# The opening of a delta-rule and feed-forward kernel, rearranged

## The chip, the cores and the metric

The kernel runs on one core of a Trainium2 chip. The metric is the device time of one execution in microseconds, the median over several executions. Engines are called as the profile calls them: PE (matrix products; PEld is its weight load), DVE (vector), ACT (scalar), POOL (GpSimd) and SP (which only issues DMAs). ACT, POOL and SP each have a DMA queue that they issue to in program order.

## The reference

For 4 batches, 8 heads and 768 steps of 48 dimensions, a delta rule is run over time, and its output goes through a feed-forward layer that takes the maximum of three products:

```python
k_n = k / (np.linalg.norm(k, axis=-1, keepdims=True) + 1e-06)
for t in range(S):
    kt, vt, bt = (k_n[:, :, t], v[:, :, t], beta[:, :, t, None])
    y[:, :, t] = np.einsum('bhd,bhde->bhe', q[:, :, t], state)
    v_old = np.einsum('bhde,bhd->bhe', state, kt)
    state = state + bt[:, :, :, None] * np.einsum('bhd,bhe->bhde', kt, vt - v_old)
...
x = attn_out.transpose(0, 2, 1, 3).reshape(B * S, H * D)      # 3072 x 384
h = np.maximum(np.maximum(x @ w1, x @ w2), x @ w3)            # 3072 x 768
out = h @ w_out                                               # 3072 x 384
```

## The kernel before

**Tiling.** Time is cut into 12 chunks of 64 steps (C = 64), and each chunk into two halves (BL = 32) and four quarters (HB = 16). A chunk has two units of work: unit n holds chunk n // 2 and half of the batches. Four units (two chunks) make a group m, of which there are six; a group is also one tile of 512 tokens of the feed-forward layer. All sums are in 32-bit floats.

**Within a chunk.** The steps depend on each other through a triangular system. `turn` transposes keys (part 0) or queries (part 1) of a unit on PE and evicts them to `kqt`; `gram` multiplies keys by keys (`at`) or keys by queries (`pt`); `keys` is gram of the keys alone. `solve(m)` inverts the diagonal blocks on DVE, one column of all blocks per two instructions (the lines L617 and L621). For group 0 the blocks are quarters of 16, because FINE = 1, and their inverses are then joined to halves of 32 and to the chunk by small products on PE. The order of these, with PE's tile name and line, is

- `halves_z` (p_e, L740): keys times the second quarters of the solution, evicted to z (L743)
- `halves_u` (p_f, L751): t times z, negated into the solution's tile `ut` (L755). t is the solution transposed, made by `halves_t` with three DVE transposes of `ut` (L700, L702)
- `turn_t1` (L685, L687): DVE transposes of the first half, to t1
- `join_z` (p_z, L768) and its evictions (L772), then `join_u` (p_j, L781), negated into `ut` (L783)
- `new` (p_u, L826): the chunk's updates u; `to_y` (p_y, L868): its output y; `to_x` (p_x, L887): y transposed into `xt` (L894), the tokens of the feed-forward layer
- `step` (p_s, L849) with the addition on DVE (L856): the state `st`; `old_k` (p_k, L798) and `old_q` (p_q) of the next chunk multiply by that state.

`heads_of` and `negated_of` deal out a stage's PSUM tiles and the engines that evict them: for chunk 0 in two parts of four heads, for later chunks in one. Their PSUM tiles (`ps_two`) come from a pool of three. `placed(cc, i, copy, part)` copies a block of the transposed solution `xs[0]` into `ut`; part is the first or the second quarter.

**Weights.** The three input weights and the output weight come as 64-bit values and are converted in 24 pieces. `fetch` asks for a piece (384 KB) on a queue; `weights()`, drawn by `some(conv, n)`, makes the two halves of a piece with three ACT instructions (L255 to L257, about 0.5 us each) per draw; `joined` finishes it with a shift on DVE (L266) and an addition on POOL (L270). `join_last` does that for a piece whose ACT part is done.

**Order.** The scheduler is off (`manual_schedule`): every engine's order is the order of the calls in the program. The opening is written out line by line, to the first feed-forward product (p_h, L1303); after it each of the feed-forward layer's products is followed by pieces of the recurrence that tables name. The solution is drawn in steps, `some(solving, n)`: for group 0 one step up to the scaling, 15 columns, and one that transposes and places the result and ends.

`busy(n, ident)` issues n products of the identity that nobody reads (p_w, L1377).

## Time and profile before

| | |
|---|---|
| median of 3 runs | 502.3 us (500.78, 502.30, 502.41) |
| the profiled execution | 501.92 us, of which the span (first to last instruction) is 500.0 us |
| mean granted PE clock | 0.976 |
| PE busy | 480.2 us, 96% of the span |
| DVE, POOL, ACT busy | 348.8, 196.1, 169.6 us |
| the solution of group 0 on DVE (L617, L621) | 16.29 to 25.21 us |
| first feed-forward product (p_h) | starts at 44.06 us |

Times are microseconds from the span's start. A line of the timeline has the start, the busy time, the engine, the source line, the operation with its tiles and shapes, the number of instructions merged into it, and in brackets how long the engine had been idle before it and what ended that. A line of the chain of waits has the start, the length, and the work or wait that led there. A window's line has the length, the busy time of each engine, the granted PE clock (1.00 is full speed) and the share of the DMA engines' time. PE's 32-bit products each leave two records.

### The profile page before, as it was taken

The numbers are of one execution on the slowest core, as the hardware profiler recorded it, in microseconds if no ns is written. First come the engines' busy times: TensorE is split into PE (matmuls) and PEld (weight loads), VectorE is DVE, ScalarE is ACT, GpSimd is POOL, SyncE is SP. The second block draws the span as 40 slices with busy tenths as digits, with TensorE's granted clock in tenths as the row PEclk, the third lists the DMA queues.
The fourth block names the chain that finished last, engine by engine and source line by source line (L and its number), as shares of the span: only waits on it lengthen the run. The fifth ranks groups of instructions, "written<-read, shape, count | busy, mean of one in ns | idle before, by whom it ended". The sixth has DMA issues, their size and how long they took to land.

```text
span 500.0 us, 18781 instructions
## 1 busy us (share of the span) xinstructions
PE 480.2 (96%) x8100; PEld 343.4 (69%) x8100; DVE 348.8 (70%) x819; ACT 169.6 (34%) x329; POOL 196.1 (39%) x330
## 2 busy tenths in 40 slices
PE   7869799999999999999999999999999999999997
PEld 6658688878665556565555565565797457988896
DVE  4888898656697352979552998565998864468753
ACT  5686665985330153201243200252211032212310
POOL 6557684764670394780575870601000020000000
PEclk9767899999999999999999999999999999999999
DMA  8948979874351655543775552833223330330001
GB/s 107 168 100 220 211 178 137 199 218 77 81 144 34 140 117 121 138 126 88 155 129 120 146 135 65 176 50 93 65 68 79 61 72 19 86 77 15 1 16 49
DMA packets 110114, 53.51 MB, mean 107 GB/s; under 512 B 93264, under 2 KB 103920, under 8 KB 110032
## 3 DMA queue, kind: packets, MB, share of 16 engines
q1 hardware_dynamic: 98528, 32.01, 31.8%
q0 software_dynamic: 9088, 19.72, 15.8%
q8 instruction: 64, 1.05, 0.9%
q10 hardware_dynamic: 2416, 0.59, 0.7%
q14 instruction: 18, 0.15, 0.1%
HBM read 39.17 MB, written 13.11 MB: 105 GB/s over the span
## 4 chain that ended last, share of the span: by engine, by line
PE 88%; DVE 3%; DMA 2%; ACT 2%; issue 2%; POOL 1%; SPq 1%; DVEq 0%; POOLq 0%; ACTq 0%
PE p_h L1303 34%; PE p_o L1346 13%; PE p_o L1040 10%; PE p_g L443 5%; PE p_c L1241 4%; PE p_u L826 3%; PE p_y L868 3%; PE p_k L798 2%; PE p_m L960 2%; PE p_t L366 2%; PE p_q L798 2%; PE p_s L849 2%; PE p_j L781 2%; PE p_z L768 2%; PE p_e L1241 1%
## 5 line engine op out<-in xcount | busy, mean ns | idle before, releaser
L1303 PE MATMUL p_h<-xt,w_sb 128*128 128x512 f32 (+1 forms) x468 | 177.7, 523 | 0.6 <-ACT xt L894 0.3
L1303 PEld LDWEIGHTS p_h<-xt,w_sb 128*128 128x128 f32 x468 | 85.1, 191 | 62.0 <-issue 53.0
L1317 DVE TENSOR_TENSOR h<-h,p_h 128x512 f32<-128x512 f32 (+1 forms) x42 | 23.9, 569 | 55.9 <-PE p_h L1303 53.4
L617 DVE TENSOR_TENSOR tmp<-x_bl,y_bl 128x31 f32<-128x31 f32 (+20 forms) x139 | 50.3, 362 | 4.0
L621 DVE TENSOR_TENSOR y_bl<-y_bl,tmp 128x31 f32<-128x31 f32 (+20 forms) x139 | 46.5, 334 | 4.8
L1346 PE MATMUL p_o<-wo_sb,h 128*128 128x384 f32 x144 | 49.2, 490 | 0.4 <-POOL wo_sb L270 0.4
L1313 ACT ACTIVATE h<-p_h 128x512 f32<-128x512 f32 (+1 forms) x30 | 16.6, 552 | 76.2 <-PE p_h L1303 76.2
L401 POOL DMA_DIRECT2D turned<-in_q_dram x72 | 39.2, 552 | 5.1 <-POOL turned L396 2.6
L1346 PEld LDWEIGHTS p_o<-wo_sb,h 128*128 128x128 f32 x144 | 26.8, 190 | 18.5 <-POOL wo_sb L270 1.0
L443 PEld LDWEIGHTS p_g<-kqt 48*64 48x64 f32 x1184 | 23.5, 138 | 11.5 <-issue 7.1
L443 PE MATMUL p_g<-kqt 48*64 48x64 f32 (+1 forms) x1184 | 26.7, 238 | 2.9 <-ACT kqt L372 2.9
L270 POOL TENSOR_TENSOR w_sb<-mant,up 128x384 int32<-128x384 int32 x18 | 18.5, 1032 | 23.7 <-DVE mant L266 20.0
L1352 ACT COPY o_sb<-p_o 128x384 f32<-128x384 f32 x12 | 5.7, 478 | 61.7 <-PE p_o L1346 41.7
L396 POOL MEMSET turned<- 128x96 f32 x18 | 3.3, 190 | 59.1 <-DVE kqt L417 59.1
L653 POOL DMA_DIRECT2D ut<-y_d x4 | 2.6, 651 | 60.4 <-DMA y_d<-y_bl 60.4
L148 POOL DMA_DIRECT2D v_t<-in_v_dram x14 | 11.6, 830 | 28.7 <-PE p_u L826 28.7
L856 DVE TENSOR_TENSOR st<-st,p_s 48x768 f32<-48x768 f32 (+1 forms) x18 | 17.1, 951 | 7.7 <-PE p_s L849 7.3
L810 DVE TENSOR_TENSOR v_t<-v_t,p_k 128x768 f32<-128x768 f32 x11 | 10.4, 949 | 15.3 <-PE p_k L798 15.3
L1346 PE MATMUL p_o<-w_sb,xt 128*128 128x384 f32 x60 | 21.0, 486 | 0.0
L427 DVE TENSOR_TENSOR pt<-p_g,mask 128x512 f32<-128x512 f32 x20 | 13.7, 689 | 10.4 <-PE p_g L443 10.3
L460 ACT COPY at<-p_g 128x512 f32<-128x512 f32 x22 | 12.7, 583 | 18.8 <-DVE pt L427 16.5
L401 POOL DMA_DIRECT2D turned<-in_k_dram x32 | 17.5, 553 | 3.0 <-DMA v_t<-in_v_dram 1.9
(252 smaller groups left out, 917.4 us busy)
## 6 DMA issues: line engine op xcount, KB each, us to landing
w_bits<-in_moe_w_dram SPq DMA_DIRECT2D x9, 384.0 KB, 5.3
w_bits<-in_moe_w_dram POOLq DMA_DIRECT2D x9, 384.0 KB, 4.8
turned<-in_q_dram POOLq DMA_DIRECT2D x72, 48.0 KB, 2.6
out_dram<-o_sb SPq DMA_DIRECT2D x34, 96.0 KB, 2.3
y_x<-y SPq DMA_DIRECT2D x32, 96.0 KB, 2.3
qall<-y_x SPq DMA_DIRECT2D x32, 96.0 KB, 2.9
v_t<-in_v_dram POOLq DMA_DIRECT2D x14, 192.0 KB, 4.5
at_d<-at SPq DMA_DIRECT2D x76, 32.0 KB, 2.9
```

The costliest lines, as they stand in the source:

```text
L270: nc.gpsimd.tensor_tensor(out=dst.bitcast(I32), in0=mant_v.bitcast(I32), in1=up_v, op=ALU.add)
L401: (queue, nc.gpsimd)[i].dma_start(out=t[p0 : p0 + 32, bb, at : at + NP * 2 * D].rearrange("p (j x) -> p j x", j=NP), in_=(k, q)[i][2 * bb ...
L443: nc.tensor.matmul(p_g[rows(bb ^ (g * i)), par, c0 : c0 + C * (1 + whole)], kq[:, 0], kq if whole else kq[:, i],)
L617: nc.vector.tensor_tensor(out=t_v, in0=row.to_broadcast(t_v.shape), in1=column.to_broadcast(t_v.shape), op=ALU.mult,)
L621: nc.vector.tensor_tensor(out=rest, in0=rest, in1=t_v, op=ALU.subtract)
L798: nc.tensor.matmul(p_b[rows(bb), par, c0 : c0 + D], kqt[g][dims(par), j, bb ^ g, i], st[dims(par), bb ^ g, g, j],)
L856: nc.vector.tensor_tensor(out=s_v[r], in0=s_v[r], in1=p_s[r, :, 0 : H * D], op=ALU.add)
L1040: nc.tensor.matmul(to[:, g], a[j][:, 128 * g : 128 * (g + 1)], b[j], start=(start and g == of[0] and j == 0), stop=(stop and g == of[-1] a ...
L1241: nc.tensor.matmul(to, w[stays], moves, start=(n == 0), stop=(n == len(terms) - 1))
L1303: nc.tensor.matmul(p_h, w_sb[i][:, t, f * 128 : (f + 1) * 128], xt[:, t, lo : lo + w], start=(t == 0), stop=(t == KT - 1),)
L1317: nc.vector.tensor_tensor(out=h, in0=h, in1=p_h, op=ALU.max)
L1346: nc.tensor.matmul(p_o, stays, moves, start=(n == 0), stop=(n == len(terms) - 1))
```

## The change

It concerns the opening (group 0) alone, but for the way conversions are drawn and for the products of `join_z` in chunk 1.

- t of chunk 0 is no longer made by transposing `ut`. One DVE transpose of the solution itself (`corners`, into the free tile t1[1]) gives the first quarters, and eight small copies (`corner`) put them into t, which POOL has cleared before: three on DVE, three on POOL, two on ACT. The second quarter of `ut` is placed first (two copies on POOL, two on ACT), the corners follow, and the first quarter is placed after p_e has been issued.
- `weights()` yields after each ACT instruction. A draw of before is three draws now, and in the opening the single steps stand between evictions. Two pieces may wait for their join (`held`), and the third piece uses a part of the output weight's tile as scratch.
- `warmed` puts products of the identity into a stage's PSUM tile ahead of its own ones: two in p_e, p_z and p_y, one in p_f, p_j and p_u, nine in all.
- `join_z` of chunks 0 and 1 multiplies all 64 rows of keys in place of 32, and evicts each part in one copy in place of two.
- z's parts of p_e and p_z are all evicted on ACT; p_f's second part is negated by DVE alone; the second half of xt of chunk 0 is copied by DVE.
- The first queries are asked for on POOL's queue, earlier; the fourth ones inside the solution; weight pieces one at a time, between the stores of the keys' products.
- The solution's last step of before is gone from `solve`; the draw of 16 steps that stands in the opening now has 15 columns to draw and reaches the two stores that the other groups make (`y_d`).
- The order of the calls is new: the queries' turns and products stand earlier.

The core of the diff:

```diff
+            if n == 2:
+                mant, up = (
+                    in_wo(1).rearrange("p s r -> p (s r)")[:, lo : lo + 384].bitcast(t)
+                    for lo, t in ((0, U32), (384, I32))
+                )
...
             nc.scalar.mul(mant_v.bitcast(FP32), high.bitcast(FP32), 2.0**-112)
+            yield
             nc.scalar.mul(halves[0], low, 2.0**-29)
+            yield
             nc.scalar.mul(halves[1], high.bitcast(FP32), 2.0**-64)
-            join_last()
+            if len(waiting) > held[0]:
+                join_last()
...
+    def turned_back(part):
+        nc.vector.transpose(
+            out=in_rows(xs[0])[:, part],
+            in_=solved[0].rearrange("p c i -> p i c")[:, part],
+        )
+    def corners():
+        by_column = t1[1].rearrange("p g h x -> p (g h x)").rearrange(
+            "p (c x) -> p c x", x=BL
+        )
+        nc.vector.transpose(out=by_column, in_=solved[0][:, 0:HB])
+        return by_column
+    def corner(by_column, i, g, copy):
+        bb, half = divmod(i, 2)
+        copy(
+            fine[0][g][block(bb ^ g, half), :, BL * half : BL * half + HB],
+            by_column[block(bb, half), :, H * g : H * (g + 1)].rearrange(
+                "p c h -> p h c"
+            ),
+        )
...
         if m in (0, 2):
             nc.gpsimd.memset(y_bl, 0.0)
+            if m == 0:
+                load_q(3, (nc.gpsimd, nc.gpsimd))
...
-        if m == 0:
-            bl_0.append(k_bl)
-            back, ahead = in_rows(xs[0]), y.rearrange("p c i -> p i c")
...
-            for part, copies in (
-                (slice(HB, BL), (P, A, P, A)), (slice(0, HB), (V, P, V, A)),
-            ):
-                nc.vector.transpose(out=back[:, part], in_=ahead[:, part])
-                for i, copy in enumerate(copies):
-                    placed(0, i, copy, part)
-            yield
-            return
...
+    def warmed(p, n):
+        for _ in range(n):
+            nc.tensor.matmul(p[:, 0, 0:128], ident, ident)
+        return p
+    AHEAD = dict(p_e=(2, 0), p_f=(1, 0), p_z=(2, 0), p_j=(1, 0), p_u=(1, 0), p_y=(2, 0))
...
-        yield range(NP), (p[0], p[0]), (nc.scalar.mul,) * 2
-        yield range(NP, H), (p[1], p[2]), (nc.scalar.mul, nc.vector.tensor_scalar_mul)
+        for i, engines in enumerate(((A, A), (V, V) if name == "p_f" else (A, V))):
...
+                    if c < 2 * FINE:
+                        nc.tensor.matmul(
+                            p_v[rows(bb ^ g), g, i],
+                            at[g][rows(bb), h],
+                            second[rows(bb), g, h],
+                        )
+                        continue
...
-    some(solving, HB + 1)
-    for copied in scores:
-        copied()
-    halves_t(0)
+    some(solving, HB)
+    first, second = slice(0, HB), slice(HB, BL)
+    turned_back(second)
+    of_first = corners()
+    for i, copy in enumerate((P.tensor_copy, A.copy, P.tensor_copy, A.copy)):
+        placed(0, i, copy, second)
+    for i in range(4):
+        for g, engine in enumerate((V if i < 3 else A, P if i < 3 else A)):
+            corner(of_first, i, g, engine.copy if engine is A else engine.tensor_copy)
+    turned_back(first)
     halves_z(0)
```

More of the change, by code (lines that the diff above doesn't have):

```diff
@@ L228, in fetch @@
             fetched[0] += 1
-    waiting = []
+    waiting, held = deque(), [2]
     def join_last():
         if waiting:
-            joined(*waiting.pop())
+            joined(*waiting.popleft())
     def weights():
@@ L242, in weights @@
                 join_last()
-                yield
+                for _ in range(3):
+                    yield
             bits = staged.popleft().rearrange("p (a b two) -> p a b two", a=a, two=2)
             low, high = bits[:, :, :, 0], bits[:, :, :, 1]
-            mant = work.tile([128, 384], U32, name="mant", bufs=2)
-            up = work.tile([128, 384], I32, name="up", bufs=2)
+            if n == 2:
[3 more added lines that the diff above has]
+                )
+            else:
+                mant = work.tile([128, 384], U32, name="mant", bufs=2)
+                up = work.tile([128, 384], I32, name="up", bufs=2)
             mant_v = mant.rearrange("p (a b) -> p a b", a=a)
@@ L255, in weights @@
             nc.scalar.mul(mant_v.bitcast(FP32), high.bitcast(FP32), 2.0**-112)
+            yield
             nc.scalar.mul(halves[0], low, 2.0**-29)
+            yield
             nc.scalar.mul(halves[1], high.bitcast(FP32), 2.0**-64)
-            join_last()
+            if len(waiting) > held[0]:
+                join_last()
             waiting.append((dst, mant, mant_v, up_v))
@@ L557, in placed @@
         copy(to[:, :, part], of[:, :, part])
+    solved = []
+    def turned_back(part):
[17 more added lines that the diff above has]
+        )
     def solve(m):
@@ L586, in solve @@
             (nc.vector if m == 1 else nc.gpsimd).tensor_copy(diagonal(y), bl)
-        if m < 3:
+        if 0 < m < 3:
             norm(k_bl, nt, root)
@@ L599, in solve @@
         nc.vector.tensor_tensor(out=xb, in0=xb, in1=by, op=ALU.mult)
+        if m == 0:
+            solved.extend((y, lambda: norm(k_bl, nt, root)))
+            bl_0.append(k_bl)
         yield
@@ L626, in solve @@
             yield
-        if m == 0:
-            bl_0.append(k_bl)
-            back, ahead = in_rows(xs[0]), y.rearrange("p c i -> p i c")
-            A, V, P = nc.scalar.copy, nc.vector.tensor_copy, nc.gpsimd.tensor_copy
-            for part, copies in (
-                (slice(HB, BL), (P, A, P, A)), (slice(0, HB), (V, P, V, A)),
-            ):
-                nc.vector.transpose(out=back[:, part], in_=ahead[:, part])
-                for i, copy in enumerate(copies):
-                    placed(0, i, copy, part)
-            yield
-            return
         y_d = dram.tile([2, 2, B, H, BL, BL], FP32, name="y_d")
@@ L702, in halves_t, with heads_of @@
             nc.vector.transpose(out=dst[1][rows(1 - bb)], in_=src[1][rows(bb)])
-    def heads_of(c, name, w):
-        copies = (nc.scalar.copy,) if c else (nc.scalar.copy, nc.vector.tensor_copy)
+    def warmed(p, n):
[3 more added lines that the diff above has]
+    AHEAD = dict(p_e=(2, 0), p_f=(1, 0), p_z=(2, 0), p_j=(1, 0), p_u=(1, 0), p_y=(2, 0))
+    def heads_of(c, name, w, copies=(nc.scalar.copy, nc.vector.tensor_copy)):
+        if c:
+            copies = (nc.scalar.copy,)
         n = H // len(copies)
         for i, copy in enumerate(copies):
-            p_v = ps_two(name)[:, :, 0 : n * w]
+            p_v = warmed(ps_two(name), 0 if c else AHEAD[name][i])[:, :, 0 : n * w]
             yield (
@@ L720, in negated_of @@
             return
-        p = [
-            ps_two(name)[:, :, 0 : NP * w].rearrange("p g (h x) -> p g h x", x=w)
-            for _ in range(3)
-        ]
-        yield range(NP), (p[0], p[0]), (nc.scalar.mul,) * 2
-        yield range(NP, H), (p[1], p[2]), (nc.scalar.mul, nc.vector.tensor_scalar_mul)
+        A, V = nc.scalar.mul, nc.vector.tensor_scalar_mul
+        for i, engines in enumerate(((A, A), (V, V) if name == "p_f" else (A, V))):
+            p = [
+                warmed(ps_two(name), AHEAD[name][i])[:, :, 0 : NP * w].rearrange(
+                    "p g (h x) -> p g h x", x=w
+                )
+                for _ in set(engines)
+            ]
+            yield range(i * NP, i * NP + NP), (p[0], p[-1]), engines
     def span(hs):
@@ L735, in halves_z @@
         second = ut[c % NU].rearrange("p g h (f two x) -> p g h f two x", two=2, x=HB)
-        for hs, p_v, copy in heads_of(c, "p_e", BL):
+        for hs, p_v, copy in heads_of(c, "p_e", BL, (nc.scalar.copy,) * 2):
             for i, h in enumerate(hs):
@@ L763, in join_z @@
         z, second = zs[c % NU], ut[c % NU][:, :, :, BL:C]
-        for hs, p_v, _ in heads_of(c, "p_z", BL):
+        for hs, p_v, copy in heads_of(c, "p_z", BL, (nc.scalar.copy,) * 2):
             for i, h in enumerate(hs):
                 for bb, g in TILES:
+                    if c < 2 * FINE:
[3 more added lines that the diff above has]
+                            second[rows(bb), g, h],
+                        )
+                        continue
                     r = block(bb, 1)
@@ L770, in join_z @@
                     )
+            if c < 2 * FINE:
+                copy(z[:, :, span(hs)], p_v)
+                continue
             for bb in range(2):
-                nc.scalar.copy(z[block(bb), :, span(hs)], p_v[block(bb)])
+                copy(z[block(bb), :, span(hs)], p_v[block(bb)])
     def join_u(c):
@@ L893, in to_x @@
             if not c:
-                nc.scalar.copy(xt[:, g], of[:, g])
+                (nc.scalar.copy, nc.vector.tensor_copy)[g](xt[:, g], of[:, g])
         if c:
@@ L1384 @@
     load_beta_0()
+    load_q(0, (nc.gpsimd, nc.gpsimd))
     load_k(6)
-    load_q(0)
+    load_q(1)
     load_k(7)
-    load_q(1)
     fetch(nc.sync)
@@ L1408 @@
     turn(5, (0,))
+    turn(0, (1,))
     some(solving, 1)
+    fine[0] = [square("t") for _ in range(2)]
+    zeros(*fine[0])
+    solved.pop()()
+    load_beta()
     keys(4)
+    fetch(nc.sync)
     keys(5)
+    load_v(0)
     turn(6, (0,))
-    turn(0, (1,))
-    load_q(3, (nc.gpsimd, nc.gpsimd))
-    load_v(0)
-    for _ in range(2):
-        fetch(nc.sync)
-    load_beta()
+    gram(0, (1,), None, later=True)()
     keys(6)
-    gram(0, (1,), None, later=True)()
+    fetch(nc.sync)
+    turn(1, (1,))
+    gram(1, (1,), None, later=True)()
+    turn(2, (1,))
     turn(7, (0,))
-    turn(1, (1,))
+    copied = gram(2, (1,), None, later=True)
     keys(7)
-    turn(2, (1,))
-    gram(1, (1,), None, later=True)()
+    fetch(nc.sync)
+    copied()
+    some(conv, 2)
+    turn(3, (1,))
     some(conv, 1)
-    turn(3, (1,))
-    scores = [gram(n, (1,), None, later=True) for n in (2, 3)]
-    some(solving, HB + 1)
-    for copied in scores:
-        copied()
-    halves_t(0)
+    gram(3, (1,), None, later=True)()
+    some(conv, 1)
+    some(solving, HB)
[8 more added lines that the diff above has]
+    turned_back(first)
     halves_z(0)
@@ L1435 @@
     some(conv, 1)
-    placed(1, 0)
+    for i, copy in (
+        (3, A.copy), (1, P.tensor_copy), (0, V.tensor_copy), (2, P.tensor_copy),
+    ):
+        placed(0, i, copy, first)
     scale(0, nrm_0[:, 0])
-    placed(1, 1, nc.gpsimd.tensor_copy)
-    blocks(1, nc.gpsimd)
-    for _ in range(2):
-        fetch(nc.gpsimd)
+    fetch(nc.gpsimd)
     halves_u(0)
+    some(conv, 1)
     turn_t1(0)
     join_z(0)
-    placed(1, 2)
+    join_last()
+    masked(pts[0], by_par(pts[0]))
+    blocks(1, nc.gpsimd)
+    some(conv, 1)
     join_u(0)
-    for n in range(2):
-        masked(pts[n], by_par(pts[n]))
+    masked(pts[1], by_par(pts[1]))
+    join_last()
+    fetch(nc.gpsimd)
     old_k(0)
@@ L1451 @@
     new(0)
-    some(conv, 1)
-    fetch(nc.gpsimd)
+    placed(1, 0)
+    placed(1, 1, nc.gpsimd.tensor_copy)
+    some(conv, 2)
+    to_y(0)
+    join_last()
     load_v(1, nc.gpsimd)
+    placed(1, 2)
+    busy(2, ident)
+    to_x(0)
+    busy(1, ident)
     placed(1, 3)
-    to_y(0)
-    busy(2, ident)
-    join_last()
+    held[0] = 0
     halves_t(1)
@@ L1461 @@
     some(solving, 1)
-    to_x(0)
-    busy(1, ident)
-    some(conv, 1)
+    some(conv, 3)
     LINKS = {
@@ L1568 @@
         if i in CONVERTED:
-            some(conv, 1)
+            some(conv, 3)
         if i == 0:
```

## The prediction

> **What bounds the kernel now.** I read the page first (busy time, the slices), then the chain of waits in order of time, then the timeline of 25 to 62 us, and last the windows of one regular width.

> ```profile
> PE 480.2 (96%) x8100; PEld 343.4 (69%) x8100; DVE 348.8 (70%) x819; ACT 169.6 (34%) x329; POOL 196.1 (39%) x330
> PE   7869799999999999999999999999999999999997
> ```

> PE is the bound: after the fourth slice it has next to no idle time. The opening (the first four slices, up to the first feed-forward product at 44.06) is where PE waits, so a microsecond taken from the opening is worth one at the end as long as nothing after 44 us holds PE back. The chain in order of time shows who leads in the opening:

> ```profile
> 26.48 0.68 ACT ut L557
> ...
> 29.18 0.71 DVE t L700
> 29.92 0.70 DVE t L702
> 30.66 0.71 DVE t L702
> 31.39 0.43 DVE z L743
> ...
> 37.30 2.18 PE p_u L826 x64
> 39.48 1.79 PE p_y L868 x56
> 41.26 1.15 PE p_w L1377 x4
> ...
> 44.06 2.86 PE p_h L1303 x12
> ```

> To be seen: the solution ends on DVE at 25.21; from there 18.85 us pass to p_h, 2.1 of them in the three transposes L700/L702 that the change drops. From 37.3 on it is PE itself, at half its rate, as 3.41 us windows show (columns: length, busy PE, PEld, DVE, ACT, POOL, PEclk, DMA):

> ```profile
> 12.43:15.84 3.41, 1.77 (x68) 1.47 (x68) 3.16 (x6) 2.79 (x8) 1.85 (x3) 1.00 1.11 171
> 22.67:26.08 3.41, 2.45 (x74) 1.91 (x72) 3.07 (x11) 3.26 (x7) 0.00 (x0) 1.00 0.77 141
> 26.08:29.49 3.41, 2.16 (x96) 1.86 (x96) 2.81 (x5) 3.34 (x7) 1.89 (x3) 1.00 1.09 261
> 36.32:39.73 3.41, 3.14 (x119) 2.84 (x116) 2.23 (x5) 2.25 (x7) 2.00 (x3) 0.50 0.62 196
> 39.73:43.14 3.41, 3.41 (x65) 3.32 (x61) 2.99 (x7) 2.33 (x6) 2.23 (x3) 0.50 0.56 196
> ```

> The granted clock changes only at such window ends: down at 15.84 and 29.49 after windows 52% and 63% busy, not down after 72%, up at 43.14 after 100%, not up after 92%. Right after the opening there is one more stop, in the timeline of PE:

> ```profile
> 51.96 1.02 PE L798 MATMUL p_k<-st,kqt 48*64 48x48 f32 x55
> 55.37 0.37 PE L798 MATMUL p_k<-st,kqt 48*64 48x48 f32 x9 [2.38 <-issue]
> ```

> It waits for nothing in the program; a 16 KB packet of the instruction queue falls into it (52 us), among DMA engines that are full. And p_k starts 0.2 us after the state update L856 on DVE ends (51.91), so DVE has no slack there either.

> **The change part by part**, from the end of the solution (25.21).

> Before it: the fourth queries' two DMA issues (1.44 on POOL in the row of 18.18) now stand between the clearing of y_bl (ends 14.05) and the diagonal copy that starts the solution; they wait for the first queries' transposes and end about 15.5, and the copy starts at 15.57 now: 0 to 0.3, I take 0.1. The two clearings for t on POOL (half of the 0.98 of L570 each) run beside DVE's steps: in the 0.1. The first queries are asked for 4 to 6 us earlier on POOL's queue, so PE's 1.68 us wait at 14.8 (they landed late) goes. ACT then has 11 evictions of 0.55 and 4 conversion steps of 0.5 ahead of the first placed copy, against 10 and 3: 15.4 + 8.0 = 23.5, plus its waits for PE (3.8 in the rows, less the 1.8 for those queries) = 25.5. The copy can start at 26.35, when the first transpose is done. So ACT is just in time: nothing, with up to 1.5 if PE runs at half rate. The second weight is converted ahead of the copies too; its load must have landed. It landed at 29.36 behind the values, and is now asked for ahead of them: 0, at worst 3.0.

> p_e thus starts where it did, 27.95. Its second half no longer waits 0.39 behind two score evictions: ends 29.3, was 29.67.

> f's transposes: the three (2.1) give way to one transpose of the solution (0.71) and eight corner copies: three on DVE (0.29 as L525's), three on POOL, two on ACT (0.26). No row has POOL's form; between L506's 0.46 and L557's 0.65, 0.5. POOL ends at 27.7 + 1.5 = 29.25, DVE earlier. p_f starts at 29.45 (last z eviction 0.39 on ACT; a product of 0.58 in front is hidden), where its bulk started at 31.42. At 2.1 for 64 it ends 31.55, was 33.33.

> Negations: the second half's four now all go to DVE, 4 x 0.31 = 1.25 in place of two beside two on ACT: p_z starts 32.8, was 34.13.

> p_z takes 64 rows in place of 32: 1.08 becomes 2.1 at half clock (as p_f), 1.1 at full (as L740 at 46.85). Two full-height evictions replace four of 0.36 in a row on ACT: z done 35.2, was 36.41. With one new product ahead of p_j and a conversion step (0.56) ahead of its negations: p_u starts 37.1, was 37.30. Most of the gain is spent here on the 64 rows.

> The unread products: nine stand new on PE, in front of p_e, p_f, p_z, p_j, p_u and p_y; 0.58 each at half clock (1.15 for two, L1377), 0.3 at full. All but the two of p_y fill waits. They are what changes the clock: from 29.45 PE has gaps of 0.2 in all, so the window 29.5 to 32.9 is 96% busy and 32.9 to 36.3 is 100%. By the rows the rise then comes at 36.3, not 43.14.

> From p_u: 1.25 (row 110.46, full clock) + 0.6 (two products) + 1.08 (row 67.93) + 0.56 (y on DVE, 40.6) + 1.5 = 42.1. The 1.5 is DVE: a mantissa shift 0.35 and a placed copy 0.6 are queued ahead of the second xt copy (0.56), which moved there from ACT. That placed copy took 1.22 beside POOL at 35.44: 0.6 more at worst. Was 44.06: 2.0 earlier. POOL's joins and the load of the next blocks come in a new order (the load is issued near 38.7 instead of 36.14, and lands 3.8 later, at 42.5, ahead of DVE's first step on it near 44.8); the third weight's join ends near 42.2, and p_h needs it 1.4 after its start, at 43.5. Both cost nothing, and the second up to 1 if POOL is late.

> Then p_k. DVE's halves_t(1) starts 2.1 after y, at 42.7, was 42.20, so the state is ready at 52.4, and PE waits there. But its instructions are asked for 2 us earlier as well (p_s comes earlier), so the 2.38 stop falls into this wait: p_k ends at 53.7, was 55.74. The gain stays 2.0. In ffn(0) the conversions take the same three steps per piece; nothing else moves.

> Also, 16 steps of the solution are drawn where 15 are left: two stores of y_bl (256 KB each) go out on SP that nobody reads. SP is idle from 31 to 45, the DMA engines are full to 29.5 and nearly idle to 36: 0, at worst 0.5 for a load behind them.

> Sum: the profiled execution took 501.92 (span 500.0, 1.92 around it), 0.4 under the median of 502.3 (runs 500.78 to 502.41). 501.92 - 2.0 = 499.9; against the median 500.3. I give 500.0.

> [...]

> **Rivals.**
> - *Earlier rise*: a 96% window is enough, and full clock from 32.9. p_z, p_j take 1.1 each, p_u starts 36.1, p_h 41.1: 499.0. For it: nothing between 92% and 100% was seen. Against: 92% didn't do. 0.12.
> - *Half clock to the end of the opening* (slower). No window is full before p_u, because the score products run at half rate too, in a bad place of the window. Then eleven batches of 1.06 and two waits of 0.6 keep ACT till 28.0, the placed copies end at 29.3, p_e starts 1.5 late, p_u at 38.6; p_u to p_h takes 2.18 + 1.15 + 2.0 + 0.56 + 1.5 = 7.4 against 6.76: p_h at 46.0, and DVE's state late by as much: +1.9, 503.8 to 504.2. For it: half clock 10 of the first 40 us now, and a gap of 5 us before p_e stays. Against: the queries' wait that brought the first fall goes. It turns to a loss when p_e starts after 29.9 or the rise comes after 39.7. 0.25.
> - *The stop in p_k stays where it is*, since the packet waits on full DMA engines and not on PE: p_k ends at 55.4, 0.3 earlier: 501.6. For it: the loads there hang on DVE's and ACT's steps, not on PE's. Against: the first of them is then asked for earlier too. 0.15.
> - *The second weight lands late* and holds ACT: +1 to +3, 503 to 504.9. 0.06.

> **How the numbers follow.** Forecast 0.42, 500.0, its own range 498.5 to 501.2. A measurement of this kernel tells about 0.3% (1.5 us) from no change. Faster by more: 0.42 + 0.12 = 0.54; within: 0.15; slower: 0.25 + 0.06 = 0.31. The range reaches down to the earlier rise without the fall at 56.8 (1.7 less, half of 3.4 at half rate): 497.3, and up to the late weight: 497 to 505.

> **What would show it.** Right: p_e at 28, p_f at 29.5, granted clock 1.00 from 36 to 40, p_h at 42, PE idle before p_k and not inside it. Wrong: ACT's placed copies after 28; granted clock 0.50 under p_u; a stop labelled issue inside p_k that ends at 55; p_x's second copy late on DVE.

## The result: slower by 1%

The changed kernel takes 506.65 us (median; 504.72, 505.88, 507.42, 508.82), the kernel before 501.83: a ratio of 1.010, interval 1.0052 to 1.0147. The forecast was 500.0, with a range of 497 to 505. Run again beside the experiments it is at 1.009 (1.0058 to 1.0122). The profiled execution is the fastest of the four: 504.72 us, span 503.0, 3.0 longer than the span before. Ratios, here and below, compare fast executions alone; the few slow ones (one at a granted clock of 0.65 took 695 us) are left out of them.

**The profile after.** The two rows of the page:

```profile
PE 482.1 (96%) x8118; PEld 345.5 (69%) x8118; DVE 350.1 (70%) x821; ACT 169.1 (34%) x326; POOL 199.9 (40%) x337
PE   6789799989999999999999999999999999999996
```

PE still has next to no idle time after the opening, and the third slice (25 to 38 us) is fuller than before (8 for 6), in part by work that nobody reads. The chain of waits in order of time:

```profile
27.52 1.92 PE p_e L779 x60
29.44 0.72 PE p_f L734 x2
30.16 1.86 PE p_f L790 x64
32.02 1.15 PE p_z L734 x4
33.17 1.86 PE p_z L808 x64
35.04 0.72 PE p_j L734 x2
...
37.22 0.79 PE p_u L734 x2
38.01 1.89 PE p_u L876 x64
39.90 1.15 PE p_y L734 x4
41.05 1.89 PE p_y L918 x64
...
44.68 0.56 DVE xt L944
...
45.98 0.71 DVE t L728
...
54.61 0.87 DVE st L906
...
55.53 1.15 PE p_k L848 x64
```

To be seen: the unread products (L734) stand in the chain itself, at half rate, between the end of one stage and the start of the next. After them the chain runs over DVE, whose state update is 3.6 us later than before (55.49 for 51.91). The windows of 3.41 us (length, busy PE, PEld, DVE, ACT, POOL, PEclk, DMA):

```profile
22.44:25.85 3.41, 1.34 (x36) 1.08 (x36) 3.07 (x11) 2.90 (x6) 0.00 (x0) 1.00 0.70 121
...
29.26:32.68 3.42, 3.42 (x73) 3.07 (x72) 0.73 (x3) 2.93 (x8) 3.28 (x4) 0.50 0.85 221
32.68:36.09 3.41, 3.41 (x98) 2.90 (x100) 2.94 (x8) 1.71 (x4) 1.04 (x2) 0.50 0.64 202
...
39.50:42.91 3.41, 3.41 (x85) 3.00 (x81) 1.74 (x2) 1.58 (x4) 1.70 (x2) 0.50 0.39 123
```

The clock falls at 25.85, one window earlier than the fall at 29.49 before (the short fall at 15.84 is gone): the score products were moved ahead, and PE has 1.34 us of work left in the window that ends there. It does not rise after two windows in which PE is busy from end to end, only after a third one, at 42.91. The last view is the timeline of PE behind the opening:

```profile
55.53 1.15 PE L848 MATMUL p_k<-st,kqt 48*64 48x48 f32 x64 [2.75 <-DVE st L906]
...
67.24 0.91 PE L876 MATMUL p_u<-v_t,ut 64*64 64x48 f32 x46 [1.06 <-issue]
...
106.53 0.31 PE L815 MATMUL p_z<-ut,at 32*32 32x32 f32 x11 [1.18 <-issue]
...
126.39 1.24 PE L1353 MATMUL p_h<-xt,w_sb 128*128 128x256 f32 x5 [0.66 <-issue]
```

The stop of 2.38 inside p_k is gone: PE waits 2.75 for the state instead. New stops that wait for nothing in the program stand in p_u, p_z and p_h; the kernel before has none above 0.4 from 60 to 140 us.

### The profile page after: what moved, and what is told of

The parts are those of the page before. It is cut to its first block, busy times and chain, and to the rows that moved or that the text cites. A ratio compares the mean times of both kernels' runs of the same rounds, so it can differ in the third digit from the quotient of the medians.

```text
span 503.0 us, 18827 instructions
## 1 busy us (share of the span) xinstructions
PE 482.1 (96%) x8118; PEld 345.5 (69%) x8118; DVE 350.1 (70%) x821; ACT 169.1 (34%) x326; POOL 199.9 (40%) x337
## 3 DMA queue, kind: packets, MB, share of 16 engines
q0 software_dynamic: 9072, 19.52, 15.4%
## 4 chain that ended last, share of the span: by engine, by line
PE 90%; DVE 5%; issue 1%; POOL 1%; DMA 1%; ACT 0%; SPq 0%; DVEq 0%; POOLq 0%
PE p_h L1353 33%; PE p_o L1396 13%; PE p_o L1090 12%; PE p_c L1291 5%; PE p_g L453 4%; PE p_u L876 3%; PE p_y L918 3%; PE p_k L848 2%; PE p_m L1010 2%; PE p_q L848 2%; PE p_s L899 2%; PE p_j L831 2%; PE p_t L376 1%; PE p_z L815 1%; PE p_e L1291 1%
## 5 line engine op out<-in xcount | busy, mean ns | idle before, releaser
L1367 DVE TENSOR_TENSOR h<-h,p_h 128x512 f32<-128x512 f32 (+1 forms) x42 | 23.9, 570 | 57.4 <-PE p_h L1353 53.8
L657 DVE TENSOR_TENSOR tmp<-x_bl,y_bl 128x31 f32<-128x31 f32 (+20 forms) x139 | 49.2, 354 | 4.0
L661 DVE TENSOR_TENSOR y_bl<-y_bl,tmp 128x31 f32<-128x31 f32 (+20 forms) x139 | 48.4, 348 | 4.8
L280 POOL TENSOR_TENSOR w_sb<-mant,up 128x384 int32<-128x384 int32 x17 | 17.5, 1034 | 20.5 <-DVE mant L276 20.0
L906 DVE TENSOR_TENSOR st<-st,p_s 48x768 f32<-48x768 f32 (+1 forms) x18 | 17.1, 951 | 7.5 <-PE p_s L899 7.1
L437 DVE TENSOR_TENSOR pt<-p_g,mask 128x512 f32<-128x512 f32 x20 | 13.7, 690 | 10.4 <-PE p_g L453 10.4
L876 PEld LDWEIGHTS p_u<-v_t,ut 64*64 64x64 f32 x768 | 13.5, 142 | 7.8 <-issue 7.4
```

What stands on the lines that cost most here:

```text
L280: nc.gpsimd.tensor_tensor(out=dst.bitcast(I32), in0=mant_v.bitcast(I32), in1=up_v, op=ALU.add)
L657: nc.vector.tensor_tensor(out=t_v, in0=row.to_broadcast(t_v.shape), in1=column.to_broadcast(t_v.shape), op=ALU.mult,)
L661: nc.vector.tensor_tensor(out=rest, in0=rest, in1=t_v, op=ALU.subtract)
L876: nc.tensor.matmul(p_v[rows(bb ^ g), g, i], ut[c % NU][rows(bb), g, h], rhs[rows(bb), g, h],)
L1367: nc.vector.tensor_tensor(out=h, in0=h, in1=p_h, op=ALU.max)
```

## The experiments

Three theories were told apart. **P**: the unread products lie on the path. **C**: the clock, lost one window earlier, is the loss. **S**: nine more products move every later product nine places on in PE's instructions, and so move the stops. The table has for each kernel the ratio to the kernel before in the same series, and from its one profile the start of p_h, the stops labelled issue from 60 to 140 us (those of 0.2 us or more, added up), and the time at half clock (without the last few us of the span). "Places" is how many products more PE has issued when p_h starts than without any of the nine.

| kernel | places | ratio (95%) | p_h | stops | half clock |
|---|---|---|---|---|---|
| before | 0 | 1 | 44.06 | 0.75 | 23.9 |
| after | 9 | 1.010 (1.0052–1.0147) | 45.38 | 3.28 | 20.5 |
| after_again | 9 | 1.0090 (1.0058–1.0122) | 45.19 | 2.59 | 30.7 |
| no_ahead | 0 | 0.9997 (0.9964–1.0031) | 44.17 | 0.42 | 30.7 |
| dve_early | 9 | 1.0055 (1.0023–1.0088) | 45.22 | 2.72 | 20.5 |
| warm | 22 | 1.0072 (1.0039–1.0106) | 46.44 | 3.60 | 20.5 |
| no_ahead_dve2 | 0 | 1.0016 (0.9979–1.0054) | 46.15 | 1.57 | 20.5 |
| fill_k | 0, then 9 | 1.0080 (1.0052–1.0108) | 42.75 | 2.60 | 20.5 |
| before_ahead | 9 | 1.0118 (1.0071–1.0164) | 45.86 | 1.49 | 27.3 |
| pad9 | 9 | 1.0020 (0.9988–1.0052) | 43.10 | 3.86 | 13.6 |
| align9 | 9 | 1.0050 (1.0018–1.0082) | 42.86 | 3.52 | 27.3 |
| after_align | 64 | 1.0104 (1.0063–1.0145) | 51.23 | 1.16 | 23.9 |
| after_align2 | 1 | 1.0062 (1.0033–1.0091) | 46.13 | 1.26 | 23.9 |
| fill0 | 0 | 0.9984 (0.9955–1.0012) | 43.45 | 1.25 | 17.1 |
| fill0_again | 0 | 0.9977 (0.9948–1.0006) | 42.87 | 1.08 | 13.7 |
| fill0_m4 | −4 | 0.9983 (0.9951–1.0015) | 41.77 | 1.22 | 20.5 |
| fill0_p16 | 16 | 1.0059 (1.0031–1.0087) | 46.42 | 1.39 | 20.5 |

Executions of one kernel differ by some 2 us either way, and the clock's windows lie elsewhere in each profile (1.5 us apart in the two of the changed kernel); so the ratios judge, and the profiles explain. The stops differ by as much between profiles of kernels at one place: 0.42 in no_ahead and 1.57 in no_ahead_dve2, both at place 0.

**after_again.** The changed kernel, unchanged. 

> The changed kernel itself, once more, beside the three runs below. Its four runs so far lie between 504.72 and 508.82. If the loss is where the profile has it (p_h 1.3 late, p_k's end 0.95 late, stops of PE on instructions at 67, 106 and 126), this profile shows the same delays within 0.5 us and the median is 505 to 507. If the phase of the 3.41 us clock windows decides, the fall at 25.85 and the rise at 42.91 lie elsewhere by up to 3.4 us, and p_h starts anywhere from 42 to 47.

Median 507.31, just over the forecast. The starts of p_h (45.19) and p_k (55.34) are within 0.2 of the first profile. The windows lie 1.5 us earlier, and four of them after p_h are at half clock in place of one.

**no_ahead.**

```diff
-    AHEAD = dict(p_e=(2, 0), p_f=(1, 0), p_z=(2, 0), p_j=(1, 0), p_u=(1, 0), p_y=(2, 0))
+    AHEAD = dict(p_e=(0, 0), p_f=(0, 0), p_z=(0, 0), p_j=(0, 0), p_u=(0, 0), p_y=(0, 0))
```

> The changed kernel without the nine unread products ahead of p_e to p_y. Theory P (the products lie on the path): in the profile after, the product of p_f, that of p_j, that of p_u (0.72 each at half clock) and the two of p_y (1.15) stand between the end of one stage and the start of the next, so p_u starts about 2 us earlier than 38.0 and p_h 2 to 3 us earlier than 45.4, if the weights allow it; the time falls by 1 to 3 us against the changed kernel. Rival C (the products hold the clock): without them the windows are emptier, the half clock lasts past 42.9, by one or more windows of 3.41 us, and the time stays within 1 us or grows. Rival D (DVE's order sets the state): p_h comes earlier, but halves_t and the state update do not by more than y does; p_k's end moves by less than 2 us.

Median 501.61, 5.7 under the changed kernel: more than P, C or D gives, and the whole loss. p_u starts at 36.53, 1.4 to 1.9 earlier, p_h only 1.0 to 1.2; the clock falls at 23.35 here and stays down until 43.83, which is what C has for the clock. So there was something beyond the opening: the stops are 0.42 in place of 2.6 to 3.3.

**dve_early.**

```diff
     some(conv, 2)
+    join_last()
+    placed(1, 2)
     to_y(0)
-    join_last()
     load_v(1, nc.gpsimd)
-    placed(1, 2)
     busy(2, ident)
+    placed(1, 3)
     to_x(0)
     busy(1, ident)
-    placed(1, 3)
...
-                (nc.scalar.copy, nc.vector.tensor_copy)[g](xt[:, g], of[:, g])
+                nc.scalar.copy(xt[:, g], of[:, g])
```

> The changed kernel with the shift and addition of the third weight and one placed copy of chunk 1 ahead of the output product, the other placed copy ahead of p_x, and both halves of xt copied by ACT, so that halves_t of chunk 1 is no longer behind the xt copy on DVE. Theory D (DVE is late because these three stand behind p_y and p_x): halves_t starts at 44.2 to 44.5 in place of 45.98, the state update ends about 1.5 to 2 earlier than 55.49, p_h is not held by the third weight (45.35 before); the time falls by 1 to 2 us against the changed kernel. Rival (a stop of PE on instructions returns to the place, as the 2.38 us stop in p_k before): p_k starts earlier but ends at 55.5 to 56.5 all the same, and the time changes by less than 0.5 us.

Median 505.30, 2.0 less. In the profile D holds: halves_t starts at 44.20, the state is ready at 53.71, and p_k starts at 53.76 with a wait of 1.09 in place of 2.75. The gain itself is not clear of noise (1.0055 for 1.0090).

**warm.** Four products of the identity (`busy(4, ident)`) ahead of the last score product, and AHEAD 7, 2, 4, 2, 2, 1. 

> The changed kernel with more unread products: four ahead of the last score product (in PE's wait of 2.0 us at 21.8), seven ahead of p_e in place of two, and 2, 4, 2, 2, 1 ahead of p_f, p_z, p_j, p_u, p_y in place of 1, 2, 1, 1, 2. Theory C (the loss is the half clock from 25.85 to 42.91, and the clock falls when too few columns pass through the array in a window): the window that ends near 25.9 is full enough, the clock stays at 1.00, p_e to p_y take 1.1 to 1.25 in place of 1.9, p_u starts 2 to 3.5 us earlier than 38.0 and p_h at 40 to 43; the time falls by 2 to 5 us against the changed kernel, if the third weight does not hold p_h (it would be its addition on POOL near 44). Theory P (products cost what they take): p_f's and p_z's extra products lie on the path, p_u no earlier than 38, the time is 0 to 2 us longer.

Median 505.96. The clock held for one window more (fall at 29.80), p_e took 1.12, but from within p_f on it was down and p_u started at 39.75: the extra products lay on the path, as P says. The ratio (1.0072) is no higher than that of after_again, so P's loss of time is not seen in it.

**no_ahead_dve, no_ahead_dve2.** Both edits together. 

> Both edits that gained by themselves (no unread products: 501.6; DVE's copies earlier: 505.3; the changed kernel 507.3 beside them). If they add, 499.5 (507.3 - 5.7 - 2.0), faster than the kernel before by about 2. If the products' loss and DVE's loss are the same loss (the state update is late in both), about 501.

Median 504.58, not 499.5; the gains do not add. The profile that is read is that of a second series. 

> No unread products and DVE's copies earlier, once more, for a profile at the ordinary clock: the first one fell in an execution of 695 us at a granted clock of 0.65, and the median of the others was 504.6 where either edit alone led to expect 499.5. Rival a (with the state early, PE reaches p_k before its instructions and stops there as in the kernel before): p_k starts near 52 to 53, a stop labelled issue of 2 to 2.7 inside it or right ahead, and its end near 55.5. Otherwise: other stops of 1 us or more between 60 and 140, or one more half-clock window; the place is to be read.

```profile
54.80 1.03 PE L848 MATMUL p_k<-st,kqt 48*64 48x48 f32 x56 [0.92 <-DVE st L906]
58.01 0.33 PE L848 MATMUL p_k<-st,kqt 48*64 48x48 f32 x8 [2.17 <-issue]
```

Rival a it is (timeline of PE): with the state early (a wait of 0.92 in place of 2.75) the stop of the kernel before is back, 2.17 us at record 56 of 64 (there 2.38 at 55). The two series (1.0050 and 1.0016) give no better than no_ahead.

**fill_k.** No products in the opening, nine in p_k's tile: `p_b = warmed(ps_two(name), 9)` for p_k of chunk 1. 

> The changed kernel with its nine unread products all moved from ahead of p_e to p_y into p_k's tile, where PE waits 2.70 for the state. Theory S (the nine products move every later product by nine places in the instruction blocks, and so bring stops of PE at 67, 106 and 126, 3 us in all): the opening is as without products (p_h near 44.2), but the stops return behind p_k (1 us in p_u, 1 us in p_z, 0.4 to 0.7 in p_h), and the time is 503.5 to 504.5. Theory P (only their place in the opening costs): 501 to 502 as without products, with at most 0.4 us at each of those stops. Theory C beside both: the window before p_k is fuller, so the half clock that followed it (54 to 64 without products) goes, 2 to 3 us less: 499 to 500 with P, 501.5 with S.

```profile
52.90 2.27 PE L734 MATMUL p_k<-ident 128*128 128x128 f32 x18 [2.75 <-DVE st L906]
```

The nine did not fill the wait: they started only when the state was done, and took 2.27 behind it. So this run did not part S from P. But its stops are those of S (1.12 in p_z, 0.66 in p_h), and a half-clock window follows the one in p_z (105.7 to 109.1).

**before_ahead.** The kernel before with `warmed` ahead of the same stages. 

> The kernel before with the nine unread products alone, ahead of the same stages. Theory P: they lie on the path at half clock there too; p_f's and p_z's are hidden by waits of 0.3 to 0.8, p_j's, p_u's and p_y's are not (2.6 us at half clock): p_h at 45.5 to 46.5 in place of 44.06, and the time is 503.5 to 506. Rival C (they raise the clock earlier, and the loss of the changed kernel is in its new order): 500 to 502.

Median 507.89: the nine products alone cost the kernel before as much as the whole change does, or more, and more than P's 506. p_h is 1.8 late, p_z stops for 0.86, p_g for 0.63. p_k still stops, for 2.68, but after its record 37 and not 55: 18 records sooner, for nine products.

**pad9.** `busy(4, ident)` ahead of the last score product and AHEAD 5, 0, 0, 0, 0, 0. 

> The changed kernel with its nine unread products all in PE's two waits before p_e: four ahead of the last score product (a wait of 2.0), five ahead of p_e (a wait of 1.7), none later. Theory S: the stops at 67, 106 and 126 are as in the changed kernel (3 us more than without products), p_h at 43 to 44: 503.5 to 504.5. Theory P: nothing on the path but what p_e's five take beyond the wait: 501 to 502. Theory C: the window up to 25.9 holds some 2000 columns in place of 1000, the clock falls one window later (29.3), p_e and p_f run at full clock, 1 to 1.5 us earlier: 500 with P, 502.5 with S.

Median 503.92, beside 502.34 for the kernel before. The ratio of 1.0020 is nearest to S with C, which had 502.5 where the kernel before took 501.7. The clock falls at 30.85, p_e takes 1.12, and p_h is 2.1 to 2.3 earlier than in the changed kernel. Against no_ahead p_h is 1.1 earlier, but the stops are 3.4 longer, and the ratio is no lower.

**align9.** No unread products, and ahead of p_e nine that cost next to nothing:

```diff
+    def tiny(p, n):
+        for _ in range(n):
+            nc.tensor.matmul(p[0:32, 0, 0:32], ident[0:32, 0:32], ident[0:32, 0:32])
```

> The changed kernel without the nine unread products (501.6), but with nine very small ones (32 by 32, 32 columns, together about 0.3 us) in p_e's wait of 1.9 us: nothing on the path and hardly a column more for the clock, only every later product of PE stands nine places further on in its instructions. Theory S (the place in the instruction blocks brings the stops): stops near 67, 105, 118 and 126 as in the four kernels with nine more products (2.6 to 3.9 us in all from 60 to 140, against 0.4 without them), and 503.5 to 505. Theory P (only the time of the products in the opening counts): 501 to 502, stops under 0.5.

Median 505.64; the ratio is 0.53% (2.7 us) above that of no_ahead. Nothing was added to the path: p_h starts at 42.86, earlier than there. The timeline of PE at p_z of chunk 3, first no_ahead, then align9:

```profile
105.03 1.35 PE L815 MATMUL p_z<-ut,at 32*32 32x32 f32 x128
106.30 2.86 PE L1353 MATMUL p_h<-xt,w_sb 128*128 128x256 f32 x12
```

```profile
104.26 1.25 PE L821 MATMUL p_z<-ut,at 32*32 32x32 f32 x117
106.89 0.31 PE L821 MATMUL p_z<-ut,at 32*32 32x32 f32 x11 [1.38 <-issue]
107.12 4.54 PE L1359 MATMUL p_h<-xt,w_sb 128*128 128x256 f32 x12
```

The changed kernel stops after the same 117 records. Without the nine places (18 records) that point comes 7 records into p_h, some 1.7 us later (p_h takes 0.24 a record), and no stop is seen there. A half-clock window follows the stop: the p_h behind it takes 4.54 in place of 2.86, at half clock from 107.7 to 111.1.

**after_align.** The changed kernel and 55 such small products, 64 places in all. 

> The changed kernel with its nine unread products where they are, and 55 very small ones (1 to 2 us together, in p_e's wait of 1.1 to 1.7) ahead of them, so that PE's later products stand 64 places further on than without any, which is one block of instructions and so the same place in a block. Theory S: the stops from 60 to 140 fall back to 0.5 us or so, the opening stays as late as it is (p_h near 45.3, up to 1 later): 504 to 505.5, against 507.3. Theory P: the stops do not matter or stay, 507 to 508.

```profile
28.22:31.63 3.41, 3.41 (x70) 3.41 (x67) 3.23 (x6) 1.95 (x4) 2.47 (x5) 0.50 0.70 160
```

The 55 took 5.26 us (48 ns a record, most of them at half clock), not 1 to 2, and p_h starts at 51.23, 5.9 later. So neither forecast came, but the time is only 0.7 us higher by the ratios (1.0104 for 1.0090): the stops fell to 1.16, with none at p_z. The window shown holds little but these products: PE is busy throughout, and the clock does not rise.

**after_align2.** The same unread columns at the same places, in fewer products.

```diff
-        for _ in range(n):
-            nc.tensor.matmul(p[:, 0, 0:128], ident, ident)
+        if n:
+            nc.tensor.matmul(p[:, 0, 0 : 128 * n], ident, wide[:, 0 : 128 * n])
...
-    busy(6, ident)
+    busy(1, clear[:, 0:512])
+    busy(1, clear[:, 512:768])
...
-    busy(2, ident)
+    busy(1, wide[:, 0:256])
```

> The changed kernel with the same unread columns at the same places, in fewer products: two of 128 columns become one of 256 (in p_e, p_z, p_y, and of the three around p_x the first two), and the six at the start become one of 512 and one of 256. From p_x on PE's products stand one place further than without the nine, not nine. Theory S with P: the path in the opening stays as slow as it is (p_h near 45), the stops from 60 to 140 fall from 2.6 to 3.3 us to about 1, and the ratio to the kernel before falls from 1.009 to 1.004 or so. If the place in the blocks is nothing: 1.008 to 1.010.

Median 505.48, ratio 1.0062 for 1.0090: 1.4 us from the place alone, with p_h no earlier (46.13), though the two intervals overlap. No stop is left at p_z or at p_h near 126.

**fill0, fill0_again, fill0_m4, fill0_p16.** No unread products but one of 512 columns in each of PE's two waits before p_e, and one of 256 in place of the three around p_x; then the same four places back (fewer at the start) and sixteen on (16 small ones).

```diff
+    busy(1, wide)
     gram(3, (1,), None, later=True)()
...
+            if c + i == 0 and name == "p_e":
+                nc.tensor.matmul(p_two[:, 0], ident, wide)
...
-    busy(2, ident)
+    busy(1, wide[:, 0:256])
     to_x(0)
-    busy(1, ident)
```

> The changed kernel with the array kept at work in the two waits before p_e by one product of 512 columns in each, none ahead of p_f to p_y, and one product of 256 columns in place of the three around p_x: PE issues as many products before p_h as without any of the nine, less one at p_x and plus none, so the instruction blocks are those of 501.6. Theories S and C together: the clock falls one window later than without products (near 29 to 31 in place of 23 to 26), p_e and p_f take 1.1 to 1.3, p_h starts near 43, the stops from 60 to 140 stay under 0.8 us: 499.5 to 500.5, faster than the kernel before. If only S holds: 501 to 502. If C costs elsewhere (the state is still late on DVE, PE waits for it before p_k and a half-clock window follows): 501.

> The kernel of two long products before p_e once more (0.9984 of the kernel before, interval 0.9955 to 1.0012), beside the two that shift it by -4 and +16 places: 0.996 to 1.000. Above 1.001 it is no better than the kernel before.

> The kernel of two long products before p_e, with four products fewer at the start (one of 512 and one of 256 columns in place of six), so that all that follows stands four places earlier in the blocks. If the stops hang on the place and four is a small step, they lie as in the kernel with the two long products (1.0 us near 65, 1.1 near 254), each a little longer or shorter: within 0.2% of it. If small steps matter: a difference of 0.3% or more either way, with stops that the profile shows.

> The kernel of two long products before p_e, with 16 very small ones (about 0.8 us together, in PE's wait of 1.1 ahead of the last score product), so that all that follows stands 16 places further on. Theory S from the kernels nine places on (ratios 1.005 to 1.010, a stop of 0.9 to 1.4 near p_z at 105): a like loss, 0.3 to 0.7% over the kernel without them, or another place of the stops with as much in all. If nine places are a special case: within 0.2%.

fill0 is at 0.9984 and 0.9977 (medians 502.35 and 501.30 beside 503.75 and 503.23): 1.1% faster than the changed kernel, and some 0.2% faster than the kernel before, though each interval just reaches past 1. C holds in part: the clock falls at 27.6 in both (23.35 in no_ahead), and less of the opening is at half clock (13.7 for 20.5). But p_e still starts at half clock and takes 1.81, not 1.1 to 1.3, and the stops are 1.08 and 1.25, not under 0.8. Four places back changes nothing (0.9983); sixteen on costs 0.8%, and its longest stops lie in the opening (3.4 us), where p_h comes 3.0 to 3.6 later; the sixteen products themselves take 1.2 us. The timeline of PE at p_u of chunk 1, for fill0, fill0_m4 and fill0_p16:

```profile
63.72 0.78 PE L879 MATMUL p_u<-v_t,ut 64*64 64x48 f32 x35
65.54 0.67 PE L879 MATMUL p_u<-v_t,ut 64*64 64x48 f32 x29 [1.04 <-issue]
```

```profile
62.56 0.90 PE L879 MATMUL p_u<-v_t,ut 64*64 64x48 f32 x43
64.19 0.56 PE L879 MATMUL p_u<-v_t,ut 64*64 64x48 f32 x21 [0.74 <-issue]
```

```profile
32.83 0.53 PE L793 MATMUL p_f<-z,t 64*64 64x32 f32 x9 [0.75 <-issue]
...
38.54 0.42 PE L834 MATMUL p_j<-z,t 32*32 32x32 f32 x11 [1.51 <-issue]
...
43.57 0.43 PE L921 MATMUL p_y<-u,pt 64*64 64x48 f32 x12 [1.16 <-issue]
...
66.69 0.31 PE L879 MATMUL p_u<-v_t,ut 64*64 64x48 f32 x3
67.23 1.14 PE L879 MATMUL p_u<-v_t,ut 64*64 64x48 f32 x61 [0.24 <-issue]
```

p_u stops after record 35 of 64 in fill0, after 43 with four products fewer, after 3 with sixteen more, after 33 in after_align2 (one more) and after 18 in the changed kernel (nine more): two records a product. So these stops are tied to a place in PE's instructions, and not to data.

**The sum.** Taking away the place alone saves 1.4 us (after_again to after_align2), the path alone 2.0 (after_again to align9), both 4.7 (to no_ahead); counted the other way, from no_ahead, the place costs 2.7 and the path 3.3. With intervals of 0.3% on each ratio (0.45% or 2.2 us on a difference) these agree: of the 4.7, the path holds 2 to 3.3 and the place 1.4 to 2.7. The 4.7, the 2.7 and the 3.3 are clear of noise; the 1.4 and the 2.0 by themselves are not. The rest of the change is worth nothing that can be measured: no_ahead is at 0.9997 (0.9964 to 1.0031), and its p_h at 44.17 is no earlier than the 44.06 before.

## Why the prediction was wrong

*Up to p_e: right, the end by luck.* The solution ends at 24.94 (25.3 forecast). ACT's first placed copy starts at 26.07, no later than the transposed block is there, the second weight was not late, and the bulk of p_e starts at 27.52 (27.95). It ends at 29.44 (29.3), since it starts 0.4 earlier and at half rate takes 1.92 in place of 1.35.

*The transposes: right, and hidden by another term.* The three are gone from the chain, but p_f's first own product starts at 30.09 in place of 29.45, behind its unread product.

*"All but the two of p_y fill waits": this step failed.* Only those of p_e and p_z do. (From p_f's end to p_z's end it takes 3.0, and 3.2 in no_ahead.) Those of p_f, p_j and p_u (0.72 each) and of p_y (1.15) add to the chain, 3.3 us at half clock. Ahead of p_f and p_j there is no wait to fill: in no_ahead they follow at once. p_u's did not start before the negation that p_u itself waits for: 37.22, behind `ut`. A product ahead of a stage fills its wait only if it may start before the wait ends. fill_k shows the same in p_k (its nine start at 52.90, when the state is done).

*"By the rows the rise then comes at 36.3": failed.* It came at 42.91. The windows from 29.26 and 32.68 were full, as forecast, and the clock stayed down. The step took PE's busy time for what the clock goes by; in these two windows PE was busy for all of 3.42 and 3.41 us at a granted clock of 0.50, and no rise followed (the last section has a count that parts the windows better). From p_u to p_h it therefore took 7.4 us (37.94 to 45.38), the figure of the slower rival, where the forecast had 5.0.

*DVE: the order was seen, the size was not.* halves_t starts at 45.98 (42.7), and the state is ready at 55.49 (52.4). Of the 3.3 by which halves_t is late, 0.8 are there when p_u starts, 2.1 come up to y (half rate and p_y's products), 0.3 behind it. The third weight's join ends at 45.35 (42.2), behind y on DVE. The timeline names it as what p_h waited for, but it cost nothing: p_h starts 0.14 after the second half of xt (45.24), as it does in no_ahead (44.03 to 44.17), where that join ends 0.8 before p_h.

*The stop in p_k: right.* It went into the wait, as said, and no_ahead_dve2 shows that it returns when the state is earlier against PE (a wait of 0.92 in place of 2.75). So on this path DVE's lateness is worth less than it looks.

*What the sum had no term for:* the places of all later stops. The prediction used the shift for p_k alone (instructions asked for earlier) and left the stops behind it where they were. They grew from 0.75 to 3.28 us (2.59 in after_again). In after_again, fill_k and align9 a half-clock window follows the one in p_z.

*The rivals.* "Half clock to the end of the opening" came nearest: p_h at 46.0 (45.38), 503.8 to 504.2 against 504.72 in the profiled execution. Of its two conditions one came true (the rise came after 39.7, at 42.91) and one did not (p_e was not late). Its reason, that no window is full, was wrong by busy time. Its price lacked the stops, and the median lies 2.5 above it. The earlier rise did not come (two full windows from 29.26, and no rise). The stop in p_k did not stay, the second weight was not late.

## What to carry to other kernels

A product added to PE cost more than its time here: it moved every later one on in PE's program, and the stops with it (nine places on cost 0.5%, with p_h no later, from no_ahead to align9; sixteen cost 0.8% from fill0 to fill0_p16, 0.2% of it the 1.2 us that the sixteen take; four places back cost nothing). Compare it with a kernel that has as many instructions and none of the work (align9), and one that has the work in fewer instructions (after_align2). Filling waits to hold the clock did best with few long products that could start before the wait ended (fill0, at 0.9984 and 0.9977), and even there the gain over the kernel before is within the noise. And an earlier state bought nothing where PE then stopped in p_k: 2.17 us in no_ahead_dve2, at 1.0016 beside the 0.9997 of no_ahead.

## What the runs showed of the hardware

**Stops, and packets of instructions, go by some 64 products.** Two neighbouring stops in fill0, in p_u and in p_s, are 127 records apart (29 left in p_u, 4 in p_t, 6 in p_h, 64 in p_y, 24 in p_s), and as many in fill0_m4 (21, 4, 6, 64, 32): within one record 64 products of two, a record of weights beside each. The page of the changed kernel gives the instruction queue q8 64 packets of 16 KB; PE has 16,236 such records, 254 a packet. That q8 is PE's is inferred: from its first packet's start to its last one's, PE starts 126 records of products a packet, in this kernel and in the kernel before. Counted from the start of PE's program, the stops lie at the same records in all kernels: 14 of the 17 profiles have one after 1358 to 1360 records of products, and each of the 76 stops labelled issue from 46 us on ends 2.2 to 3.8 us after a packet of that queue starts. Not every such place has a stop: in align9 there is one of 1.38 after record 117 of p_z of chunk 3, in no_ahead none at that place, seven records into p_h. Nor does every stop lie among full DMA engines: in the changed kernel their share is 0.76 from 102 to 106.5, ahead of the stop of 1.18 in p_z, and 0.02 from 122 to 126.4, ahead of that of 0.66 in p_h. What makes a stop at one place and none at another was not shown.

**Small products with the same operands took longer.** 110 records of 32 by 32 products, all on rows and columns 0 to 31 of the identity, took 5.26 us in after_align: they start 33 ns apart up to the fall of the clock at 28.22, and 53 ns apart behind it. p_j's of the same size, on changing rows and columns, took 17 ns each at half clock (64 in 1.08, in the changed kernel).
